# One 64 KiB-row transfer in place of an 8 KiB-row and a 56 KiB-row transfer at the start of a streaming kernel

## The chip, the cores and the metric

The kernel runs on one core of one Trainium2 chip. The metric is the device time of one execution in microseconds (us); where several runs are given, the median is taken. Beside the times there is one profiled execution, recorded by the hardware profiler: its span runs from the first to the last instruction.

## The reference

```
B, S, D = 512, 32, 640
x, fx: bfloat16 [B, S, D];  alpha: bfloat16 [1]

def reference(x, fx, alpha):
    return x + alpha * fx
```

x, fx and the output are 20.97 MB each, so 41.94 MB are read and 20.97 MB written. There are two elementwise operations for each output element and no reuse of data.

## The kernel before, in words

Each of the three tensors is seen as 128 partitions by 81,920 elements, that is 160 "units" of 512 elements (1 KiB) a partition. In device memory the part of one partition is contiguous (160 KiB). A transfer of units a to b therefore consists of 128 rows of (b − a) KiB each, one for each partition.

On the core there is one large tile, `room`, with 207 units a partition. It can't hold x and fx whole, so its units are used again and again by a plan that is written out by hand, the string `PLAN`. Each line of it is one step, and the loop at the end of the kernel emits them in this order:

- `f a b @ at` loads units a to b of fx into room from unit `at` on; `x a b @ at` does this for x; `s a b @ at` stores units from room to the output. All of these go through `transfer` (its `dma_start` is line 96) and are issued by SyncE (SP in the profile), so there is one issue queue, in the order of the plan.
- `a` is `spread_alpha`: it loads alpha (2 bytes, line 86), and multiplies a row of 128 ones with it on TensorE (line 90), so that alpha stands in all partitions; VectorE copies it to `a_f` (line 91).
- `m t n` multiplies n units of room, from t on, by alpha in place (VectorE, line 110).
- `+ t u n` adds the n units from u on to those from t on, in place (VectorE, line 115). The result lies where x lay.
- `after + 192` on a store adds a dependency: the store is not issued before that addition is done.

A load that overwrites units waits, on SP, for the last VectorE step that read them. So the fx units 0 to 64 (room 143 to 207), x 0 to 64 and fx 64 to 128 are issued at once at the start; the next load, `x 64 88 @ 143`, waits for the first addition, which frees room 143 to 167, and so on. The stores come last. At the end, a no-op on SP waits for everything but the last store.

The first lines of the plan are the ones that matter here:

```
f 0 8 @ 143
f 8 64 @ 151
a
x 0 64 @ 0
m 143 64
f 64 128 @ 79
+ 0 143 24
x 64 88 @ 143
```

Both of the first two transfers are read by the same step, `m 143 64`.

Of the kernel before, what the change touches and what calls it, by code (L numbers as in the profile page):

```python
# [1 line left out]

# [4 lines left out]

ALU = mybir.AluOpType
F32 = mybir.dt.float32

K = 512
P = 128
ROOM = 207

PLAN = """
f 0 8 @ 143
f 8 64 @ 151
a
x 0 64 @ 0
m 143 64  # L30
# [3 lines that stand above are left out]
+ 24 167 16  # L34
x 88 104 @ 167
+ 40 183 24
x 104 128 @ 183
m 79 64
+ 143 79 17
f 128 160 @ 64  # L40
+ 160 96 7
+ 167 103 16
+ 183 119 9
x 128 160 @ 96
m 64 32
+ 192 128 9
s 0 64 @ 0 after + 192
+ 201 137 6
s 64 128 @ 143
+ 96 64 32  # L50
s 128 160 @ 96
"""


@with_exitstack
def kernel(
    ctx: ExitStack,
    tc: tile.TileContext,
    x: bass.AP,
    fx: bass.AP,  # L60
    alpha: bass.AP,
    out: bass.AP,
):
    nc = tc.nc
    whole = {
        name: t.flatten_outer_dims().rearrange("(p n) d -> p (n d)", p=P)
        for name, t in (("x", x), ("f", fx), ("s", out))
    }
    assert whole["x"].shape[1] == 160 * K

    consts = ctx.enter_context(tc.tile_pool(name="consts", bufs=1))
    psum = ctx.enter_context(tc.tile_pool(name="psum", bufs=1, space=bass.MemoryType.PSUM))
    rooms = ctx.enter_context(tc.tile_pool(name="rooms", bufs=1))
    ctx.enter_context(tc.manual_schedule())

    room = rooms.tile([P, ROOM * K], x.dtype, name="room")
    a_f = consts.tile([P, 1], F32, name="a_f")
    info = mybir.DependencyInfo(mybir.DependencyClass.Sync, mybir.DependencyReason.DATA)
    done, moved = [], {}

    def units(t, a, b):
        return t[:, a * K : b * K]

    def spread_alpha():
        a_1 = consts.tile([1, 1], alpha.dtype, name="a_1")
        done.append(nc.sync.dma_start(out=a_1[:], in_=alpha[None, :]))  # L86
        ones = consts.tile([1, P], alpha.dtype, name="ones")
        nc.vector.memset(ones[:], 1.0)  # L88
        a_ps = psum.tile([P, 1], F32, name="a_ps")
        done.append(nc.tensor.matmul(a_ps[:], ones[:], a_1[:], start=True, stop=True))  # L90
        nc.vector.tensor_copy(out=a_f[:], in_=a_ps[:])  # L91

    def transfer(what, a, b, at, after):
        away, here = units(whole[what], a, b), units(room, at, at + b - a)
        out, in_ = (away, here) if what == "s" else (here, away)
        r = nc.sync.dma_start(out=out, in_=in_)  # L96
        if after:
            tc.add_manual_dep(r.ins, moved[after].ins.name, info, reason="issued late")
        moved[what, a] = r
        done.append(r)  # L100

    for step in PLAN.strip().split("\n"):
        what, *rest = step.split()
        if what == "a":
            spread_alpha()
        elif what == "m":
            t, n = map(int, rest)
            f = units(room, t, t + n)
            done.append(
                nc.vector.tensor_scalar(out=f, in0=f, scalar1=a_f[:], scalar2=None, op0=ALU.mult)  # L110
            )
        elif what == "+":
            t, u, n = map(int, rest)
            xt, f = units(room, t, t + n), units(room, u, u + n)
            moved[what, t] = nc.vector.tensor_tensor(out=xt, in0=xt, in1=f, op=ALU.add)  # L115
            done.append(moved[what, t])
        else:
            a, b, _, at = rest[:4]
            after = (rest[5], int(rest[6])) if len(rest) > 4 else None
            transfer(what, int(a), int(b), int(at), after)  # L120

    last = nc.sync.nop(nofuse=True)
    for i in done[:-1]:
        tc.add_manual_dep(last.ins, i.ins.name, info, reason="all but the last store")


# [1 line left out]
_INS = ['x', 'fx', 'alpha']  # L128
_OUTS = [((512, 32, 640), 'bfloat16')]


# [23 lines left out]
```

## Time and profile before

| | |
|---|---|
| median of 3 runs | 150.86 us (150.72 to 150.97) |
| the profiled execution, its own time | 150.81 us |
| its span | 149.0 us |
| VectorE busy | 65.9 us, 44% of the span |
| TensorE, GpSimd busy | 0.2 us each |
| DMA queue | 1730 packets, 62.92 MB, 98.1% of 16 engines' span |
| mean rate over the span | 422 GB/s |

The span is 1.81 us shorter than the execution's own time; that part lies around the instructions that the profile shows. "Packets" are what one of the 16 DMA engines of the core moves in one go, "share of 16 engines' span" is the time that all packets took, divided by sixteen spans. In the rows of the profile, `SPq` is SyncE's instruction queue, which issues the transfers, and `room<-in_fx_dram` means a transfer from fx into `room`. The column "us to landing" runs from the issue to the last of the 16 completion signals.

### The profile page before, as it was taken

Reading aid. Unit: us, or ns where it says so; the run is one execution under the profiler, and the core shown is the slowest. Engines: PE = TensorE matmul, PEld = TensorE weight load, DVE = VectorE, ACT = ScalarE, POOL = GpSimd, SP = SyncE. Lnnn points to the kernel's source line nnn. Section 1 sums busy time; section 2 is a strip of 40 time slices with the busy share of each in tenths; the row PEclk is TensorE's granted clock in tenths of the full one; section 3 lists DMA queues with packets and bytes.
Section 4 is the critical chain, followed back from the end, with each engine's and each line's share of the span. In section 5 each row is a group of like instructions: output and inputs, shape, how many; then the busy total and the mean of one; then the engine's idle time right before and its main releaser. Section 6 shows DMA issues by size and latency. Waiting matters only on the chain.

```text
span 149.0 us, 85 instructions
## 1 busy us (share of the span) xinstructions
PE 0.2 (0%) x1; PEld 0.1 (0%) x1; DVE 65.9 (44%) x15; POOL 0.2 (0%) x4
## 2 busy tenths in 40 slices
PE   0000000000000000000000000000000000000000
PEld 0000000000000000000000000000000000000000
DVE  0000009940089998699999307969910000000000
POOL 0000000000000000000000000000000000000000
DMA  5997996969899796999998999999696969697994
GB/s 183 592 400 339 493 528 281 563 281 563 369 475 528 317 563 281 416 429 391 462 449 387 422 431 449 449 501 545 299 563 281 563 281 563 281 563 308 457 449 194
DMA packets 1730, 62.92 MB, mean 422 GB/s; under 512 B 194, under 2 KB 194, under 8 KB 194
## 3 DMA queue, kind: packets, MB, share of 16 engines
q1 hardware_dynamic: 1730, 62.92, 98.1%
HBM read 41.94 MB, written 20.97 MB: 422 GB/s over the span
## 4 chain that ended last, share of the span: by engine, by line
DMA 38%; DVE 32%; another core or an unknown queue 1%; SPq 1%; issue 0%; DVEq 0%
DMA room<-in_x_dram 38%; DVE room L115 27%; DVE room L110 6%; SPq L96 1%; SPq L86 0%; DVEq L115 0%
## 5 line engine op out<-in xcount | busy, mean ns | idle before, releaser
L115 DVE TENSOR_TENSOR room<-room 128x12288 bf16<-128x12288 bf16 (+6 forms) x10 | 43.7, 4419 | 11.5 <-DMA room<-in_x_dram 11.5
L110 DVE TENSOR_SCALAR room<-room,a_f 128x32768 bf16<-128x32768 bf16 (+1 forms) x3 | 22.0, 7330 | 9.0 <-DMA room<-in_fx_dram 9.0
L91 DVE COPY a_f<-a_ps 128x1 f32<-128x1 f32 x1 | 0.2, 159 | 21.4 <-PE a_ps L90 21.4
L88 DVE MEMSET ones<- 1x128 bf16 x1 | 0.2, 165 | 0.8 <-PEq L139 0.8
L90 PE MATMUL a_ps<-a,ones 1*128 1x1 bf16 x1 | 0.2, 159 | 22.2 <-DMA a<-in_alpha_dram 22.2
L90 PEld LDWEIGHTS <-ones 1*128 1x128 bf16 x1 | 0.1, 101 | 1.0 <-DVE ones L88 1.0
L139 POOL MEMSET const-bfloat16-1.0<- 128x1 bf16 x1 | 0.1, 101 | 0.0
L139 POOL MEMSET const-uint8-127<- 128x1 uint8 x1 | 0.1, 101 | 0.0
L139 POOL MEMSET const-float32-0.0<- 128x1 f32 x1 | 0.1, 98 | 0.2 <-issue 0.2
L139 POOL MEMSET const-float32-1.0<- 128x1 f32 x1 | 0.1, 98 | 0.0
## 6 DMA issues: line engine op xcount, KB each, us to landing
room<-in_fx_dram SPq DMA_DIRECT2D x1, 7168.0 KB, 21.1
room<-in_x_dram SPq DMA_DIRECT2D x2, 3072.0 KB, 20.7
room<-in_fx_dram SPq DMA_DIRECT2D x1, 4096.0 KB, 15.7
room<-in_x_dram SPq DMA_DIRECT2D x1, 4096.0 KB, 16.7
out_dram<-room SPq DMA_DIRECT2D x1, 4096.0 KB, 39.5
room<-in_x_dram SPq DMA_DIRECT2D x1, 2048.0 KB, 20.5
room<-in_fx_dram SPq DMA_DIRECT2D x1, 1024.0 KB, 4.6
out_dram<-room SPq DMA_DIRECT2D x2, 39.7
```

What stands on the lines that cost most here:

```text
L88: nc.vector.memset(ones[:], 1.0)
L90: done.append(nc.tensor.matmul(a_ps[:], ones[:], a_1[:], start=True, stop=True))
L91: nc.vector.tensor_copy(out=a_f[:], in_=a_ps[:])
L96: r = nc.sync.dma_start(out=out, in_=in_)
L110: nc.vector.tensor_scalar(out=f, in0=f, scalar1=a_f[:], scalar2=None, op0=ALU.mult)
L115: moved[what, t] = nc.vector.tensor_tensor(out=xt, in0=xt, in1=f, op=ALU.add)
L139: nc = _bacc.Bacc("TRN2", target_bir_lowering=False, num_devices=1)
```

## The change

The first two lines of the plan become one: fx units 0 to 64 are loaded by one transfer of 128 rows of 64 KiB, where 128 rows of 8 KiB and 128 rows of 56 KiB were loaded by two. The bytes, their places in `room` and the order of everything else stay. The other part of the diff lets the step `a` take an `after`, as stores can; the plan doesn't use it, so `late` is called with an empty list or with the same dependency as before.

```diff
 PLAN = """
-f 0 8 @ 143
-f 8 64 @ 151
+f 0 64 @ 143
 a
 x 0 64 @ 0
 m 143 64
@@
-    def spread_alpha():
+    def late(r, after):
+        if after:
+            what, a = after[1], int(after[2])
+            tc.add_manual_dep(r.ins, moved[what, a].ins.name, info, reason="issued late")
+
+    def spread_alpha(after):
         a_1 = consts.tile([1, 1], alpha.dtype, name="a_1")
         done.append(nc.sync.dma_start(out=a_1[:], in_=alpha[None, :]))
+        late(done[-1], after)
@@
         r = nc.sync.dma_start(out=out, in_=in_)
-        if after:
-            tc.add_manual_dep(r.ins, moved[after].ins.name, info, reason="issued late")
+        late(r, after)
         moved[what, a] = r
@@
         if what == "a":
-            spread_alpha()
+            spread_alpha(rest)
@@
-            after = (rest[5], int(rest[6])) if len(rest) > 4 else None
-            transfer(what, int(a), int(b), int(at), after)
+            transfer(what, int(a), int(b), int(at), rest[4:])
```

## The prediction

> **What bounds the kernel now.** I read the page first, from the busy times to the slices.
>
> ```profile
> span 149.0 us, 85 instructions
> ...
> PE 0.2 (0%) x1; PEld 0.1 (0%) x1; DVE 65.9 (44%) x15; POOL 0.2 (0%) x4
> ...
> DMA  5997996969899796999998999999696969697994
> GB/s 183 592 400 339 493 528 281 563 281 563 369 475 528 317 563 281 416 429 391 462 449 387 422 431 449 449 501 545 299 563 281 563 281 563 281 563 308 457 449 194
> DMA packets 1730, 62.92 MB, mean 422 GB/s; under 512 B 194, under 2 KB 194, under 8 KB 194
> ...
> q1 hardware_dynamic: 1730, 62.92, 98.1%
> ```
>
> VectorE works 65.9 of 149.0 us; the DMA engines work 98.1%. The ups and downs of the slices are long packets counted in one slice or the next. The packet count shows that rows are not cut: twelve big transfers of 128 rows give 1536 packets, and the 194 under 512 B are alpha and the completion signals. Next, VectorE's waits:
>
> ```profile
> DVE a_f L91 <- PE a_ps L90: 21.4, 1, 21.4
> DVE room L115 <- DMA room<-in_x_dram: 11.5, 2, 10.3
> DVE room L110 <- DMA room<-in_fx_dram: 9.0, 2, 7.1
> ```
>
> VectorE always waits for loads. The chain of waits names VectorE for 32%, but that is the chain of what released what, not of what was short: its pieces lie on top of DMA work. The timeline shows the start, with SP's issues:
>
> ```profile
> 0.72 0.85 SPq L96 DMA_DIRECT2D room<-in_fx_dram  x2
> ...
> 1.63 0.32 SPq L86 DMA_DIRECT2D a<-in_alpha_dram  x1
> 1.99 0.34 SPq L96 DMA_DIRECT2D room<-in_x_dram  x1
> 2.37 0.48 SPq L96 DMA_DIRECT2D room<-in_fx_dram  x1
> 22.22 0.16 PE L90 MATMUL a_ps<-a,ones 1*128 1x1 bf16 x1 [22.22 <-DMA a<-in_alpha_dram]
> ...
> 22.61 8.75 DVE L110 TENSOR_SCALAR room<-room,a_f 128x32768 bf16<-128x32768 bf16 x1
> 41.70 17.36 DVE L115 TENSOR_TENSOR room<-room 128x12288 bf16<-128x12288 bf16 x3 [10.34 <-DMA room<-in_x_dram]
> ```
>
> Last I took the trace's packet records themselves (start, duration, size), sixteen packets to a round, one for each engine. Means over a round, us from the span's start:
>
> ```
> 8 KiB rows   round 1..8 start  1.851 2.473 2.887 3.226 3.536 3.843 4.149 4.462
>              duration          0.660 0.398 0.321 0.313 0.311 0.309 0.309 0.309
> 56 KiB rows  round 1, 8 start  4.767 19.571   (2.115 a round)
> 64 KiB rows  x 0 64: start     21.691; fx 64 128: 41.038   (2.418 a round)
> ```
>
> The first packet begins at 1.73 and the last ends at 147.94. Following each engine's packets, the next begins where the one before ends (usually 3 ns before it); as far as packets can be told apart by engine, the largest gap is 0.18 us, once. So the DMA engines' work is a single unbroken stretch of 146.2 us, and the execution is that stretch, 1.73 us ahead of it, 1.08 us behind it (149.02 − 147.94), and 1.81 us around the span: 150.81, against a median of 150.86. Whatever doesn't shorten that stretch, or its beginning and end, changes nothing.
>
> **The change part by part.**
>
> *Per-row cost.* One engine moves eight rows of each transfer. In steady state it takes 8 × (0.309 + 2.115) = 19.39 us for 8 + 56 KiB rows, and 8 × 2.418 = 19.34 us for 64 KiB rows, with their completion packet in it. Eight packets fewer an engine: −0.05 us. This lies on the path, since the rings never drain.
>
> *The start.* The first 8 KiB row of an engine took 0.660 us on average, 0.351 over the steady 0.309; the seven others together some 0.11 over (0.457 in all by durations, 0.444 by the starts: 4.767 − 1.851 − 8 × 0.309). Is this a price of the rows or of the first moment? The excess is gone by the fourth round, which starts at 3.23 us, and no later first row shows it (first rounds of the 56 KiB rows 2.127 against 2.116, of x 2.418). So it belongs to the first 1.4 us, in which the flow fills. Long rows pass through the same moment. From below, all of it could vanish: −0.44. If only the first row's 0.351 remains, it is −0.09; if all remains, 0. From above there is no start with long rows in this trace; the nearest rows are the 64 KiB rows in steady state, of which the slowest of 512 took 2.532, 0.114 over 2.418; eight such would be +0.91. I take the middle between 0.351 and 0.444 as what stays, −0.05, since the first packet's excess looks like the time until data flows at all, and the excess of rounds two and three (0.089 and 0.012) may or may not be one of row changes.
>
> *Issue.* SP issues one transfer less, and alpha, x and fx 64 128 are issued some 0.44 us earlier (1.16 − 0.72). Worth nothing: x was issued at 1.99 and its first packet starts at 21.69. The first issue stays at 0.72, and issue to first packet is 1.01 us; the issue instruction takes 0.38 for 8 KiB rows, 0.42 for 56, 0.34 and 0.48 for 64 KiB, so row length isn't its price. The cover is 19 us of queued packets.
>
> *What loses its early landing.* The 8 KiB rows landed 4.6 us after issue, but nothing used them: the multiplication needs both transfers, and alpha, which lies behind them in the queue (its landing ends TensorE's wait at 22.22). In the changed kernel alpha again comes behind the same 64 KiB rows. If the first multiplication came late, it has 10.34 us in hand before the first addition, which waits for x.
>
> *What follows.* If the loads arrive 0.1 us earlier, all that waits for them moves with them. The closest cover is the second half's: the first store is issued at 97.25, needs about 1.01 us to start, and the load ahead of it keeps the engines busy until about 99.3, so 1.07 us are left, and the addition that releases it is itself released by a load (fx 128 160, landed at 90.18). So no hole opens that would eat the gain.
>
> Sum: −0.05 − 0.05 = −0.10 us, 150.81 − 0.10 = 150.71; I say 150.7.
>
> **A rule against the trace.** By the rows, one transfer's end costs its successor nothing: the last 8 KiB round starts at 4.462 and the 56 KiB round at 4.767, 0.305 later, which is one row's time. The Trainium skill, page "DMA: Bandwidth & Descriptors", section "Anatomy of one DMA — SWDGE (gpsimd) path", gives a fixed cost of about 2.0 us to every DMA, beside its bytes. As an estimate from that page, dropping one transfer would give 148.8 us. The trace disagrees for queued transfers; the rule returns as a rival below.
>
> **The rivals.**
>
> *Slower: the rows march in step.* The sixteen engines begin at almost the same moment (first starts 1.73 to 2.08), on rows of the same length. The 8 KiB rows make each engine change its row eight times in 2.9 us; 64 KiB rows don't for 2.4 us. If engines in step get in each other's way, and short rows loosen them, each of the eight rounds pays. Speaking for it: rounds of 64 KiB rows differ, up to a mean of 2.441 in one round of fx 64 128, 0.023 over; single rows are up to 0.114 over. Against: the durations of 56 KiB rows are flat from their second round on. At 0.023 a round, +0.18 − 0.10 gives 150.9; at 0.114 a round, +0.91 − 0.10 gives 151.6. It decides from 0.0125 a round (the gain gone), and from 0.056 a round it can be told from no change (151.16 − 150.71 = 0.45, over eight rounds). Chance 0.16.
>
> *Faster: the start's loss is a matter of rows.* If it is the short rows that hold up the first 1.4 us, all 0.44 goes with the 0.05: 150.81 − 0.49 = 150.32. For it: the second round still pays 0.089 although data flow by then. Against: most of the loss is in the very first packet. Chance 0.17.
>
> *Faster: each transfer pays its own handling.* The first transfer took 4.6 us from issue to landing, of which eight rows are 2.47; 2.1 us would go: 148.7. Against it stands the unbroken handover above. This is where the rule of the skill would lead. Chance 0.02.
>
> *The change doesn't do what it says.* If the 64 KiB rows were cut into 8 KiB packets, a row would take 8 × 0.309 = 2.472 and eight rows 19.78, 0.39 more than the 19.39 of before: 151.2; cut once, into 56 and 8 KiB, they would take 19.39 again: 150.8, the likelier of the two. The same form of transfer exists for x and isn't cut. Chance 0.03.
>
> **How the numbers follow.** A measurement of this kernel can tell about 0.2%, 0.30 us, from no change: faster means under 150.56, slower over 151.16. The forecast has 0.62; its own range, the start's term from −0.09 to 0 and the runs' spread of 0.25 us, is 150.5 to 151.0. Of it I give 0.07 to faster and 0.03 to slower. The faster rivals give 0.15 and 0.02 to faster, the rest of the first, 0.02, to same. The slower rival gives 0.13 to slower and 0.03 to same, the cut rows 0.03 to same. Faster 0.24, same 0.60, slower 0.16. The range takes in the vanishing start at the lower end and the slower rival up to a price of 0.05 a round (+0.4 − 0.1) at the upper: 150.3 to 151.1.
>
> **What would show it.** In the changed profile: 1586 packets (128 rows and 16 completion packets fewer), 178 of them under 512 B; SP's second issue at about 1.16 is alpha's; the first issue still at 0.72 and the first packet near 1.73. If I am right, the first row of each engine takes about 2.418 + 0.35 to 0.44, the next seven 2.418, alpha lands near 22.1, and x's first packets start near 21.59 (21.691 − 0.10); all later steps keep their distance from there to the end. The forecast is wrong if rounds two to eight of the first transfer exceed 2.43, if the first row takes under 2.6 or over 3.0, if a gap between packets appears later, or if the time moves although x's start didn't.

## The result and the profile after

The changed kernel takes 151.48 us (median of 6 runs, 151.37 to 151.59), the kernel before 150.85 (150.72 to 150.97): the ratio is 1.0042, with a 95% interval of 1.0031 to 1.0052. It is slower by 0.6 us, where 150.7 was forecast; the time lies above the range's upper end, 151.1. The profiled execution took 151.39 us against 150.81.

The page of the changed kernel (VectorE's row, the packets, the queue):

```profile
span 149.6 us, 84 instructions
...
PE 0.2 (0%) x1; PEld 0.1 (0%) x1; DVE 65.9 (44%) x15; POOL 0.2 (0%) x4
...
DMA packets 1586, 62.92 MB, mean 421 GB/s; under 512 B 178, under 2 KB 178, under 8 KB 178
...
q1 hardware_dynamic: 1586, 62.92, 97.8%
```

The change did what it says: 1586 packets, 178 small ones. VectorE's work is what it was, and the DMA queue is nearly as full as before (97.8% against 98.1%). Its waits:

```profile
DVE a_f L96 <- PE a_ps L95: 21.5, 1, 21.5
DVE room L119 <- DMA room<-in_x_dram: 11.6, 2, 10.6
DVE room L114 <- DMA room<-in_fx_dram: 9.4, 3, 7.1
```

One wait for fx is new (three times, before two). The timeline shows which:

```profile
0.73 0.38 SPq L101 DMA_DIRECT2D room<-in_fx_dram  x1
...
1.16 0.31 SPq L90 DMA_DIRECT2D a<-in_alpha_dram  x1
1.52 0.34 SPq L101 DMA_DIRECT2D room<-in_x_dram  x1
1.91 0.66 SPq L101 DMA_DIRECT2D room<-in_fx_dram  x1
22.27 0.16 PE L95 MATMUL a_ps<-a,ones 1*128 1x1 bf16 x1 [22.27 <-DMA a<-in_alpha_dram]
22.46 0.16 DVE L96 COPY a_f<-a_ps 128x1 f32<-128x1 f32 x1 [21.49 <-PE a_ps L95]
23.06 8.75 DVE L114 TENSOR_SCALAR room<-room,a_f 128x32768 bf16<-128x32768 bf16 x1 [0.44 <-DMA room<-in_fx_dram]
42.37 6.56 DVE L119 TENSOR_TENSOR room<-room 128x12288 bf16<-128x12288 bf16 x1 [10.56 <-DMA room<-in_x_dram]
```

The first issue is where it was, the others come 0.47 us earlier. Alpha is a single packet, which one engine carries behind its fx rows; it is there at 22.27, 0.05 later than before. But the multiplication now waits 0.44 us more, for fx: some other engine is far behind. The first addition starts at 42.37, not 41.70, 0.67 later, and of this 0.58 is left at the end of the profiled execution. So the delay arises in the first transfer. The packet records, means of a round of sixteen packets:

```
                                 before                      after
first packets start (mean, last) 1.851, 2.084                1.956, 2.513
round 1 over its steady time     8 KiB rows: 0.351           64 KiB rows: 3.129 - 2.418 = 0.711
rounds 2 to 8 over it            0.089 0.012 0.004 ... 0     0.006 0.002 0.002 0.002 0 0.001 0.002
x 0 64 starts (mean)             21.691                      22.003
```

And the completion signals, which the trace has for each engine: how many us the first and the last of a transfer's sixteen are apart, and when the last store's signals come, on the mean and the last of them:

```
                        fx to 64  x 0 64  fx 64 128  stores     last store: mean, last   execution
before                  0.38      0.34    0.36       0.42 0.44  148.024, 148.274         150.81
after                   0.91      0.91    0.91       0.92 0.92  148.266, 148.852         151.39
```

In both kernels the execution's own time is 2.54 us above the time of the last signal, which is counted from the span's start. The loss of 0.58 us is thus the sum of two things: the engines end 0.24 us later on average (148.266 − 148.024), and the slowest of them lies 0.586 us behind the average, where it was 0.250, which is 0.34. Both are there after the first transfer (0.30 and 0.39 at the signals of fx to 64) and are mostly still there at the end: each engine goes on with its own share of every transfer, and from the second round on a 64 KiB row takes 2.42 to 2.43 us on the mean, so the late engine does not catch up.

### The profile page after: what moved, and what is told of

Read it like the earlier page. It is cut to its first block, busy times and chain, and to the rows that moved or that the text cites. A ratio compares the mean times of both kernels' runs of the same rounds, so it can differ in the third digit from the quotient of the medians.

```text
span 149.6 us, 84 instructions
## 1 busy us (share of the span) xinstructions
PE 0.2 (0%) x1; PEld 0.1 (0%) x1; DVE 65.9 (44%) x15; POOL 0.2 (0%) x4
## 2 busy tenths in 40 slices
DMA packets 1586, 62.92 MB, mean 421 GB/s; under 512 B 178, under 2 KB 178, under 8 KB 178
## 3 DMA queue, kind: packets, MB, share of 16 engines
q1 hardware_dynamic: 1586, 62.92, 97.8%
## 4 chain that ended last, share of the span: by engine, by line
DMA 38%; DVE 32%; another core or an unknown queue 1%; SPq 0%; issue 0%; DVEq 0%
DMA room<-in_x_dram 38%; DVE room L119 26%; DVE room L114 6%; SPq L101 0%; SPq L90 0%; DVEq L119 0%
```

## The experiments

Theories after this result: the length of the rows with which the flow starts (R), the earlier issues (I), the number of transfers (N). Later ones are named with their runs. Diffs are against the changed kernel.

**Which part of the change?** The order turned round, two equal lengths, a shorter first part, and later issues:

```diff
 e1: -f 0 64 @ 143      e2: -f 0 64 @ 143      e3: -f 0 64 @ 143
     +f 0 56 @ 143          +f 0 32 @ 143          +f 0 2 @ 143
     +f 56 64 @ 199         +f 32 64 @ 175         +f 2 64 @ 145
 e4, in spread_alpha: +again = consts.tile([1, 1], alpha.dtype, name="again")
                      +done.append(nc.sync.dma_start(out=again[:], in_=alpha[None, :]))
```

> The order of the two transfers is turned round: 56 KiB rows first, 8 KiB rows second; as many transfers, packets and issues as before. Theory R (rows that are long in the first 1.4 us lose more there, and unevenly over the engines): first round about 0.7 us over its steady 2.116, spread of the engines' starts afterwards about 0.9 us, time as after, 151.4. Theory I (what costs is that alpha, x and fx 64 128 are issued 0.44 us earlier): as before, 150.85, since the second issue is a big transfer again. Theory N (number of transfers or packets matters): as before, 150.85.

> Two transfers of 32 KiB rows. Theory R: a 32 KiB row lasts 1.21 us, nearly the whole of the first 1.4 us, so close to after: 151.2 to 151.5, first round some 0.6 to 0.7 us over 1.213. Theories I and N: 150.85.

> 2 KiB rows first (eight take about 0.65 us an engine), then 62 KiB rows. Theory R in the form that the rows in flight during the whole first 1.4 us count: in between, 151.0 to 151.3, since the 62 KiB rows begin in that time. Theory R in the form that only the very first packets count (a warm-up): as before or better, 150.7 to 150.9. Theories I and N: 150.85.

> As after, with one more 2-byte load of alpha on SP behind the first, which moves the issues of x and fx 64 128 back by some 0.36 us, to about where they were before (a load of 2 bytes that isn't used is added). Theory R: 151.48 as after. Theory I: back to about 150.9.

Measured, beside 150.92 for the kernel before: e1 151.47 (ratio 1.0037, 1.0024 to 1.0049), e2 151.10 (1.0014, 1.0005 to 1.0023), e3 151.33 (1.0030, 1.0017 to 1.0042), e4 151.40 (1.0032, 1.0020 to 1.0045). e1 speaks against N and I: two transfers, the packets and issues of before, and the time of after. Its timeline and page:

```profile
0.73 0.85 SPq L102 DMA_DIRECT2D room<-in_fx_dram  x2
...
1.63 0.32 SPq L91 DMA_DIRECT2D a<-in_alpha_dram  x1
1.99 0.35 SPq L102 DMA_DIRECT2D room<-in_x_dram  x1
...
23.04 8.75 DVE L115 TENSOR_SCALAR room<-room,a_f 128x32768 bf16<-128x32768 bf16 x1 [0.36 <-DMA room<-in_fx_dram]
42.35 6.56 DVE L120 TENSOR_TENSOR room<-room 128x12288 bf16<-128x12288 bf16 x1 [10.56 <-DMA room<-in_x_dram]
```
```profile
q1 hardware_dynamic: 1730, 62.92, 97.9%
```

SP's times and the 1730 packets are those of before; the multiplication's wait (0.36) and the addition's 42.35 are those of after. The first round of 56 KiB rows took 0.745 over its 2.116, that of 32 KiB rows 0.665 over 1.213. In e3 the 62 KiB rows began at 2.59 to 3.19 us, and up to 3.214 was measured for their 2.342: a warm-up of 0.8 us with 2 KiB rows (from 1.76 on) doesn't help, long rows lose behind it too. e3 ended just above the forecast of the theory that counts the whole first 1.4 us.

e2 ended below the 151.2 to 151.5 that theory R gave it, although its first round lost what R had said. It shows the two parts of the delay separately: its last store's signals come as late on the mean as those of the changed kernel (148.289 against 148.266), but the last of them 0.27 us sooner (148.581 against 148.852), and the time is 0.38 shorter.

**How does it go with the length, and is it the program's first moment?** Two more lengths, and the same two starts in mid-kernel: x is held back until fx has landed, so that the engines stand empty.

```diff
 e5: -f 0 64 @ 143     e6: -f 0 64 @ 143     e7, e8: -f 0 64 @ 143
     +f 0 16 @ 143         +f 0 2 @ 143              +f 0 8 @ 143
     +f 16 64 @ 159        +f 2 8 @ 145              +f 8 64 @ 151
                           +f 8 64 @ 151             -x 0 64 @ 0
                                                 e7: +x 0 64 @ 0 after f 8
                                                 e8: +x 0 8 @ 0 after f 8
                                                     +x 8 64 @ 8
```

> 16 KiB rows first (0.61 us each, eight take 4.9 us), then 48 KiB rows. Theory R1 (short rows keep the flow from piling up while it starts, and the loss grows with the row's length up to about 32 KiB): between 8 and 32 KiB rows, 150.85 to 151.10, the last engine ending at 147.9 to 148.2. Theory R2 (any row over 8 KiB loses in full): 151.1 or more. Theory K (the start is the same everywhere, and what differs is chance of a build): no order in the lengths.

> Rows of 2, 6 and 56 KiB in three transfers; long rows begin at about 4.7 us, as in the kernel before. Theory R1: what went wrong with 2 and then 62 KiB rows was that long rows began inside the first 1.4 us; here they don't, so 150.75 to 150.95. Theory W (2 KiB rows at the start are bad in themselves): 151.3 as with 2 and 62.

> The kernel before, but x 0 64 is issued only when fx 8 64 has landed, so that the DMA engines stand empty for some 1.6 us and start again, with 64 KiB rows. To be read against e8_idle_8_56. Both theories: 150.85 + about 1.6 + the loss of the new start. Theory F (the loss comes whenever the flow starts from empty engines): 0.5 to 0.7 us slower than e8, about 153.3, first round of x some 0.7 us over 2.418 and the engines' ends 0.9 us apart. Theory C (only the first moment of the program is like that): equal to e8 within 0.15 us, about 152.6, first round of x near 2.418 plus at most 0.35.

> As e7_idle_64, but the new start is made by 8 KiB rows of x, and its 56 KiB rows follow. Theory F: about 150.85 + 1.6 + 0.4 = 152.8, and 0.5 to 0.7 faster than e7_idle_64. Theory C: equal to e7_idle_64 within 0.15 us.

e5 took 150.82 (1.0003, 0.9995 to 1.0012), e7 153.70 (1.0193, 1.0179 to 1.0206), e8 153.09 (1.0150, 1.0137 to 1.0164). The timelines of e7 and of e8, in this order:

```profile
22.38 0.35 SPq L102 DMA_DIRECT2D room<-in_x_dram  x1
...
44.73 6.56 DVE L120 TENSOR_TENSOR room<-room 128x12288 bf16<-128x12288 bf16 x1 [13.40 <-DMA room<-in_x_dram]
```
```profile
22.37 0.82 SPq L103 DMA_DIRECT2D room<-in_x_dram  x2
...
44.04 6.56 DVE L121 TENSOR_TENSOR room<-room 128x12288 bf16<-128x12288 bf16 x1 [12.72 <-DMA room<-in_x_dram]
```

The issue is at the same moment, the addition 0.69 us apart, the times 0.61: the change's own size, found again 22 us into the program. In e7 the first round of x took 3.064 and the completions are 0.95 us apart, after having been 0.51 apart for fx; in e8 they go from 0.47 to 0.40. So theory F holds for this second start: the loss doesn't belong to the first moment of the program. Both runs took some 0.3 to 0.4 us more than forecast: the hole was longer, as x started 2.00 us later in e7 than before (23.691 against 21.691), where 1.6 had been expected. e6 took 151.30 (1.0031, 1.0015 to 1.0046), but its median says little: five runs lie between 150.81 and 150.97, six between 151.30 and 151.82. Its long rows began at 4.53 us and later, and still one of them took 2.772 for 2.116 and the completions came out 0.89 us apart. So "no long row before 3.3 us" (theory R1) isn't the rule either. Theory W, that 2 KiB rows at the start are bad in themselves, fits e3 and e6 alike, and no run separates it from the other reading of e3.

**Is it the length alone?** Rows 64 KiB apart in memory (the first 64 units of each tensor are its first 8 MiB), two further lengths, then 128 KiB apart, and the mid-kernel start at 64 KiB:

```diff
 e9:  -name: t.flatten_outer_dims().rearrange("(p n) d -> p (n d)", p=P)
      +name: t.rearrange("a b d -> (a b d)")
      and in units, for the flat tensors:
      +cut = 64 * K * P
      +a, b, t = (a, b, t[:cut]) if a < 64 else (a - 64, b - 64, t[cut:])
      +t = t.rearrange("(p n) -> p n", p=P)
 e10: e9 with f 0 8, f 8 64        e13: e9 with 128 for 64
 e15: e9 with e7's plan            e14: e13 with f 0 8, f 8 64
 e16: e9 with f 0 16, f 16 64
 e11: f 0 4, f 4 64 alone          e12: f 0 12, f 12 64 alone
```

> As after, but the first 64 units of each tensor are its first 128 x 64 KiB (rows lie 64 KiB apart in place of 160 KiB), the other 96 units lie behind them at 96 KiB a row. Lengths and counts of packets are those of after. To be read against e10_pitch_64_8_56. Theory R (the length of the rows in the start): 0.5 to 0.7 us slower than e10, first round some 0.7 us over 2.418. Theory A (engines that read rows at certain distances get in each other's way): the difference to e10 moves by 0.3 us or more, to under 0.3 or over 0.9.

> The same placing of rows as e9_pitch_64_one, with 8 and 56 KiB rows at the start. Theory R: 0.5 to 0.7 us faster than e9, and within 0.2 us of the kernel before. Theory A: see e9.

> 4 KiB rows (about 0.16 us each, eight take 1.3 us and the start's loss on top) then 60 KiB rows, which begin at about 3.6 us. Theory R1 (what counts is that no long row begins before the flow is full, at about 3.3 us): 150.8 to 151.0, like 8 KiB rows. Theory E (the loss is smaller the longer short rows go on, evenly): between 2 KiB (151.33) and 8 KiB (150.85), about 151.1.

> 12 KiB rows, then 52 KiB rows, to see whether there is a faster place between 8 and 16 KiB, which both gave about 150.85. Theory R1: 150.75 to 150.9, no gain that can be measured, since the first packet's loss of some 0.35 us stays. If the unevenness of the engines can be brought down further: 150.6.

> As after, with the first 128 units of each tensor as its first 128 x 128 KiB: rows lie 128 KiB apart. Theory A (how far apart the rows lie decides how unevenly the engines come out of the start): unevenness of the first transfer's completions other than 0.51 (64 KiB apart) and 0.91 us (160 KiB apart), and the time moves with it, by about its change over 0.5 us at 151.0. Theory R (row length alone): 151.5, completions 0.9 us apart, and e9 was an accident of that kernel.

> The same with 8 and 56 KiB rows at the start. Both theories: mean of the first round's loss about 0.2 to 0.3 us smaller than in e13. Theory R: 0.6 us faster than e13; theory A: faster or slower than e13 as the unevenness falls out, 150.8 to 151.2.

> The experiment with idle engines and a new start by 64 KiB rows of x (153.70 at 160 KiB between rows), with rows 64 KiB apart. Theory A, if it holds at every start: completions of x 0 64 about 0.5 us apart and 153.2, 0.4 to 0.6 faster than at 160 KiB. Theory R: 153.7.

> Rows 64 KiB apart and 16 then 48 KiB rows at the start: does a start with less unevenness than the 0.4 us of the kernel before give a faster kernel? 150.7 if completions are under 0.3 us apart, as they were with 16 KiB rows at 160 KiB; 150.9 if they are 0.5 apart as in both kernels with 64 KiB between rows.

```
rows apart  start with     round 1 over steady  x 0 64 starts  completions apart  time    ratio (95%)
160 KiB     8, 56 (before) 0.351                21.691         0.38               150.85
160 KiB     64 (after)     0.711                22.003         0.91               151.48  1.0042 (1.0031, 1.0052)
128 KiB     8, 56 (e14)    0.303                21.730         0.51               150.90  1.0001 (0.9992, 1.0010)
128 KiB     64 (e13)       0.754                21.956         0.63               151.04  1.0013 (1.0005, 1.0022)
 64 KiB     8, 56 (e10)    0.197                21.646         0.52               150.95  1.0002 (0.9992, 1.0012)
 64 KiB     64 (e9)        0.609                21.881         0.51               151.01  1.0007 (0.9998, 1.0016)
160 KiB     64, mid (e7)   0.646                               0.95               153.70  1.0193 (1.0179, 1.0206)
 64 KiB     64, mid (e15)  0.668                               0.58               153.16  1.0154 (1.0140, 1.0168)
```

The two parts of the loss come apart here too. The mean start of x moves by 0.31, 0.23 and 0.24 us from short to long rows at all three distances: that part goes with the length. The unevenness doesn't go with the length alone: long rows give 0.91 and 0.95 at 160 KiB, 0.63 at 128, 0.51 and 0.58 at 64, and the time of e15 is 0.54 under e7's. That is what theory A forecast for this part, and theory R alone falls: between e9 and e10, with rows 64 KiB apart, the change can't be told from none (0.06 us). The timeline of e9 shows it in one line; the 0.44 us wait for fx isn't there:

```profile
22.63 8.75 DVE L117 TENSOR_SCALAR room<-room,a_f 128x32768 bf16<-128x32768 bf16 x1
41.90 6.56 DVE L122 TENSOR_TENSOR room<-room 128x12288 bf16<-128x12288 bf16 x1 [10.52 <-DMA room<-in_x_dram]
```

One rival to the distance is left untested. The runs at 64 and 128 KiB were made on other chips (4 and 1) than e1 to e8 (15 and 10), and long rows 160 KiB apart were not repeated there. The kernel before, measured beside each group, took 150.84 to 150.92 on all four, and at 64 KiB the two chips agree (0.51 and 0.58), but that the unevenness of a start with long rows depends on the chip isn't excluded. The two runs of each pair, e9 and e10 or e13 and e14, shared a chip.

The others: e11 150.89 (1.0004, 0.9989 to 1.0019; runs 150.76 to 151.96), e12 151.03 (1.0007, 0.9999 to 1.0015), e16 150.94 (1.0005, 0.9996 to 1.0014), with completions 0.41 us apart. e11 came out as R1 said and e12 above its 150.75 to 150.9. By the length of the first rows at 160 KiB apart, 2, 4, 8, 12, 16, 32, 56, 64 KiB give 151.33, 150.89, 150.85, 151.03, 150.82, 151.10, 151.47, 151.48. e5 had its completions only 0.23 us apart, and gains nothing by it, since the mean of its last signals came later (148.120 against 148.024). No version beats the kernel before.

## Why the prediction was wrong

*What held.* The bound (the DMA stretch without a hole), VectorE's cover, and, in the main, the claim that what is lost at the start is still there at the end. The per-row cost of −0.05 fits too, though no run measures it alone: rounds two to eight took 2.418 to 2.424. The earlier issues were worth nothing, as said; e4, which issues x at 1.79 in place of 1.52, took 151.40, inside the spread of after's runs. That a transfer's end costs its successor nothing held: e1 has one transfer more than the changed kernel and the same time. The fixed price for each DMA that the Trainium skill gives ("DMA: Bandwidth & Descriptors", "Anatomy of one DMA — SWDGE (gpsimd) path") isn't paid by transfers queued behind one another here. That section is about transfers issued by GpSimd; those of this kernel are issued by SyncE.

*The step that failed* is "The start", the term set at −0.05. It took the excess of the first packets for the time until data flows, the same for rows of any length. So the most that it let remain was the 0.444 of before, no gain and no loss; the one larger figure, +0.91 from eight slow rows of the steady state, it left to a rival. Measured on the mean: first packets start 0.105 us later (1.956 against 1.851), and 0.711 lost in the first round where 0.444 had been lost in eight, +0.267. With −0.05 that is +0.32, and x starts 0.31 later. Some 0.07 of it is given back later, so that 0.24 is left at the last store: from 21 us on, single rows took up to 0.225 too long in the kernel before (a 32 KiB row), at most 0.066 in the changed one.

*The term that was missing* is the larger one, +0.34. The prediction worked with means over sixteen engines. The end is set by the latest, and in these two kernels a lag from the start is hardly made up: completions 0.38 us apart became 0.44, and 0.91 became 0.92. The completions stood in the trace of before: the working could have said that the time hangs on the latest engine, and how much a wider start would cost, though not that it would come.

*The rival on the other side* had the direction and the place: a start of all engines together on long rows. That they get in each other's way there is not shown, and its price was another: it took eight rounds at up to 0.114. The price falls on the first round alone, 0.711 on the mean and up to 1.007 for one engine, and the later rounds are clean. That 151.48 lies between the rival's 150.9 and 151.6 is luck. Its argument against, that the 56 KiB rows of before are flat, was no argument: those rows didn't start the flow. One of the prediction's signs, a first row of over 3.0 us, is what came.

*What stays open.* Why a start with long rows costs more, and why it was more uneven with the rows 160 KiB apart, if it is the distance and not the chip. All first transfers have 128 rows, so a longer row is also a larger first transfer; no run separates the two. The Trainium skill ("DMA: Bandwidth & Descriptors", "Latency and other measured facts") knows a distance of rows that lowers the rate, at large powers of two from 512 KiB on, and puts it, unverified, to the memory's channels. No run here has such distances, and the steady rate doesn't move: a 64 KiB row takes 2.418 at 64, 128 and 160 KiB. What the runs show is a loss that lasts about one round and then leaves the engines shifted against each other. Also open are the wide runs of e6 and e11, and whether 12 KiB rows are really later than 8 and 16 (completions 0.52 us apart at x, against 0.34 and 0.24): e12's interval reaches down to no change. The unevenness is read from one profiled execution of each kernel. The same start, 8 and 56 KiB rows 160 KiB apart, gave 0.38 (before), 0.51 (e7) and 0.47 us (e8), so a difference of 0.1 us means nothing; 0.87 to 0.95 for 64 KiB rows at that distance (after, e4, e7) against 0.51 to 0.63 at the others is more than that.

## What to carry to other kernels

Where the DMA queue never runs dry, a kernel like this ends with the latest engine, and that is mostly the one that came out of the start last. So a start is judged by the last of the first transfer's completions: their mean and their spread both count. Starting from empty engines, a first transfer with short rows (8 or 16 KiB here) can be worth 0.6 us over one with 64 KiB rows; with rows 64 KiB apart, in runs on another chip, it was worth 0.06, which is nothing that can be measured. A hole in mid-kernel has the price of a start again, on top of the hole. Fewer packets are little gain by themselves: 144 fewer were worth 0.05 us by the sum, too little to be seen in the times.

## What was not expected of the hardware

The sixteen engines of the changed kernel kept their distances for 126 us: completions 0.91 us apart at 22 us and 0.92 at the end. This isn't so everywhere: in e11 the completions drew together, from 0.45 us apart at 22 us to 0.27 at 68 us, and stayed there. The execution's own time was 2.53 to 2.54 us above the time of the last completion signal in the kernels before and after and in all sixteen experiments. A start with 64 KiB rows cost 0.61 to 0.75 us in the mean first round, at the program's start and in mid-kernel, and with the first round the loss was nearly over (at most 0.011 on the mean in the second).
